# A spectral layer and an MLP on one core: the second product two steps behind its operands, eight places for the kept half, casts without priority, two reads sooner

## The chip, the cores and the metric

The kernel runs on one core of a Trainium2 chip. The metric is the time of one execution on the device in microseconds (us), the median of several runs.

## The reference

```python
X = np.fft.rfft(x, axis=1)                       # x: 8 x 3008 x 256
Yr = Xr @ w_r - Xi @ w_i + b_r                   # Xr, Xi: real and imaginary part of X
Yi = Xr @ w_i + Xi @ w_r + b_i
Yr = np.sign(Yr) * np.maximum(np.abs(Yr) - 0.01, 0.0)      # Yi likewise
y = np.fft.irfft(Yr + 1j * Yi, n=3008, axis=1).astype(np.float32)
h = y.reshape(24064, 256) @ w_in                 # 256 x 2048, float64 words
g = np.maximum(0.01 * h, h)
out = (g @ w_out).astype(np.float32)             # 2048 x 256, float64 words
```

## The kernel before

**The spectral part.** Each of the 8 batches has a transform along its 3008 positions, done as two factors (47 and 64) by matmuls. `fwd(b)` does the first factor (`stage_a`) and writes to u_dram. `mid(b)` reads that, with a table fb for each pair of columns, does the second factor (`stage_b`, psf or psh from fb and u), splits the result into a high and a low part (eh), multiplies by the complex weights, applies the soft threshold (t, zf, zh), turns back one factor (`stage_g`) and writes v_dram. `inverse` reads v_dram (vin) and does the last factor; its result y is copied into yc. In the prologue batch 0 goes through `fwd` and `mid` alone; batches 1 to 7 are streams whose pieces are put between those of the MLP, in chunks up to index 26. The last five chunks have hardly any side work.

**The MLP** runs over 24064 tokens in 32 chunks of 752. Products are in two parts, high and low (three matmuls for each product). The first product is in Strassen's form: in each of 8 steps q of a chunk, `moe_a` has 12 matmuls into four banks psh, and `moe_b` 9 more. Behind `moe_a` a copy and an add make p (tag p1), and two adds make half of gs; `moe_b` is followed by the activations of gf and the last add of gs. gf is the half of a step's result that is used at once; gs is the kept half. `parts` splits a half into gh (a cast on the scalar engine, L594) and gl (a subtraction on the vector engine, L595). For gf that stands in the block of raised priority (AHEAD = 200); for gs it is `late`, called later.

The second product is `moe_o`: for one step, one half and one half eh of the outputs, six matmuls into one of two banks pso (L612). When step 7 is in, the bank is copied to ob on the scalar engine (L618) and written out. In the first half of a chunk the groups of half 0 stand between the pieces of the first product, taken from the list `behind`; in the second half only groups of half 1 follow, with the forms of the next chunk (`forms`, L520 to L532: sums of yc, split into yhl) between them.

**Order.** A scheduler places the recorded instructions on each engine; it goes by the order in which the code records them, by `high_priority` and by `issue_after`. A tile with n places (bufs) makes its next writer wait for the last reader of the place. `early` is a region that holds weights in the prologue; `load_wout` reads w_out in pieces `raw` of 512 KB and splits them.

Of the kernel before, what the change touches and what calls it, by code (L numbers as in the profile page):

```python
# [8 lines left out]
F32 = mybir.dt.float32  # L9
# [21 lines left out]
def spectral_mlp_kernel(  # L31
# [98 lines left out]
    def load_weights():  # L130

        w = early[:, 6 * D:6 * D + 3 * NH * D + P]
        r, d, n = (w[:, k * NH * D:(k + 1) * NH * D].rearrange("p (a f) -> p a f", a=NH) for k in range(3))
        i = sb.tile([P, NH, D], F32, name="w_i", tag="yt", bufs=1)
        for t, src in ((r, w_r), (i, w_i)):
            sync.dma_start(t, src.rearrange("(a p) f -> p a f", p=P))
        dve.tensor_sub(d, i, r)
        dve.scalar_tensor_tensor(n, i, -1.0, r, ALU.mult, ALU.subtract)
        consts.update(wr32=(r,), wd32=(d,), wn32=(n,), gb32=(w[:, 3 * NH * D:],))
# [51 lines left out]
    def load_wout():  # L191
# [5 lines left out]
        def load():  # L197
            k = len(raws)
            raw = sb.tile([P, CS, 2], U32, name="raw", tag="ez"[k % 2], bufs=1)
            with tc.issue_after(reads[-1].ins):  # L200
                sync.dma_start(raw.rearrange("p (a f) w -> p a (f w)", a=n), ov[:, k * n:(k + 1) * n, :])
            raws.append(raw)
# [25 lines left out]
    XT = [("gs", NQ - 1)] * 2 + [("gg", 6)] * 3 + [("gs", NQ - 1), ("yc", 3)]  # L228

    def fwd(b):  # L230
# [5 lines left out]
        def load(c):  # L236
            cols = slice(2 * c * D, min(2 * c + 2, NS) * D)
            n = cols.stop - cols.start
            if b < NPRE:
                tag, bufs = XT[c]  # L240
                x_t[c] = [sb.tile([PA, 2 * D], F32, name="xin", tag=tag, bufs=bufs)[:, :n] for h in range(2)]
            else:
                x_t[c] = [
                    sb.tile([PA, 2 * D], F32, name=f"xin{h}", tag="uv"[h], bufs=3 - h)[:, :n] for h in range(2)
                ]
# [79 lines left out]
    def mid(b):  # L325
        ud = u_dram[b]
# [5 lines left out]
        u_t, e_t, z_t, fb_t = {}, {}, {}, {}  # L332
# [12 lines left out]

        def turns(j):
            if j < NPAIR:
                fb_t[j] = sb.tile([P, 3, N2], F32, name="fb", tag="fb")
                sync.dma_start(fb_t[j], fb[j])
# [28 lines left out]
        def proj(j):  # L378
# [4 lines left out]
            for dst, c, w in ((0, 2, "wr"), (0, 1, "wn"), (D, 0, "wd")):  # L383
# [5 lines left out]
                if c == 2:  # L389
                    kc = sb.tile([P, D], F32, name="kc", tag="kc", bufs=1)  # L390
# [9 lines left out]
            c = sb.tile([P, 2, D], F32, name="c", tag="kb" if b else "yt", bufs=1)  # L400
# [32 lines left out]
        turns(0)  # L433
# [46 lines left out]
    def inverse(pi, eh):  # L480
# [12 lines left out]
        y = sb.tile([P, CS], F32, name="y", tag="y")  # L493
# [13 lines left out]
    def forms(ci):  # L507
# [4 lines left out]
        t = sb.tile([P, 2, HT], F32, name="yt", tag="yt", bufs=1)  # L512
# [13 lines left out]
        dve.tensor_sub(t[:, 1], b22, t[:, 0])  # L526
        dve.tensor_sub(b12, b22, b12)
        yield
        split(slice(2, 4), t)
        yield  # L530
        split(slice(4, 6), y1)
        dve.tensor_sub(b11, b21, t[:, 1])  # L532
# [16 lines left out]
    def moe_a(ci, q):  # L549
# [6 lines left out]
        u = sb.tile([P, HT], F32, name="p1", tag="p1")  # L556
        g1 = sb.tile([P, 2, 2, HP], F32, name="gs", tag="gs", bufs=NQ - 1)
# [8 lines left out]
    def moe_b(ci, q):  # L566
# [7 lines left out]
        with tc.high_priority(AHEAD):  # L574
# [3 lines left out]
            parts(ci, q, 0, g0)  # L578
            g = g1[:, :, :, :HH]
            dve.tensor_add(g[:, 0], halves(c12[:, :HT]), halves(u))  # L580
        early_parts[:] = parted
# [57 lines left out]
    def moe():  # L639
# [3 lines left out]
        def next_o(eh):  # L643
            if behind:
                in_order(moe_o, *behind[0], eh)
                if eh:
                    behind.pop(0)

        for ci in range(nch):
            nxt = tokens(ci + 1) if ci + 1 < nch else iter(())  # L650
            units = 0
            for q in range(NQ):
# [9 lines left out]
                if q >= NQ - 2:  # L662
                    late(ci, q + 2 - NQ)
# [5 lines left out]
            behind += [(ci, q, 1) for q in range(NQ)]  # L669
            for q in range(NQ):  # L670
                for eh in range(NH):
                    next_o(eh)
                    if eh:
                        late(ci, q + 2)
# [4 lines left out]
        while behind:  # L679
            for eh in range(NH):  # L680
                next_o(eh)
# [29 lines left out]
    load_win(0, (sync, act))  # L711
    load_weights()
# [13 lines left out]
    m0 = Stream(mid(0), MID)  # L726
# [13 lines left out]
    for i in range(1, 17):  # L740
# [3 lines left out]
        if 5 <= i < 12:  # L744
            next(fp.gen)
    m0.finish()
# [3 lines left out]
    next(wout)  # L750
# [144 lines left out]
```

## Time and profile before

| | |
|---|---|
| runs | 2581.2, 2583.67, 2587.37 us; median 2583.67 us |
| profiled execution | 2589.46 us, of which the span is 2587.7 us |
| TensorE (PE) busy | 2455.0 us (95%), 15388 matmuls |
| vector engine (DVE) busy | 1891.2 us (73%) |
| scalar engine (ACT) busy | 1658.8 us (64%) |
| POOL busy | 248.0 us (10%) |
| first matmul of the first product | at 143.26 us |

The span is the time from the first to the last instruction in the profile. Matmuls are pipelined and their ends are modelled, so a busy TensorE isn't one at its peak; a weight load (PEld) stands ahead of each matmul or pair and shows what it waited for.

### The profile page before, as it was taken

What the parts mean: (1) busy time and instruction counts of PE and PEld (TensorE: products, weight loads), DVE (VectorE), ACT (ScalarE), POOL (GpSimd) and SP (SyncE); (2) the same over time, 40 slices, a digit from 0 to 9 for tenths busy, and PEclk for the clock granted to TensorE, in tenths of its full rate; (3) what the DMA queues carried; (4) which work ended last, traced back from release to release, by engine and by line L of the source; (5) the groups of instructions that cost most, each with busy time, mean ns of one, the idle gap of its engine ahead of it and who ended that gap; (6) DMA issues with size and microseconds to landing.
All of it is one profiled execution on the core that took longest, in us unless ns stands there. A gap on an engine that the chain in (4) does not pass through costs nothing.

```text
span 2587.7 us, 41422 instructions
## 1 busy us (share of the span) xinstructions
PE 2455.0 (95%) x15388; PEld 2336.0 (90%) x15388; DVE 1891.2 (73%) x3208; ACT 1658.8 (64%) x3198; POOL 248.0 (10%) x192
## 2 busy tenths in 40 slices
PE   6879999999999999999999999999999999999999
PEld 4569999999899998999989999899999999999998
DVE  6687788677776777777777767777768777766665
ACT  4666676667566666676656766566766666655554
POOL 0200012000110001100011001100002000000000
PEclk8989999999999999999999999999999999999999
DMA  7531123221231212321123211321213221100000
GB/s 234 164 119 54 49 56 114 71 57 51 71 95 53 57 45 76 86 66 49 49 81 86 57 53 44 93 79 51 60 50 100 65 59 40 44 28 28 17 13 19
DMA packets 138479, 173.68 MB, mean 67 GB/s; under 512 B 15661, under 2 KB 100645, under 8 KB 138277
## 3 DMA queue, kind: packets, MB, share of 16 engines
q1 hardware_dynamic: 97688, 124.17, 16.0%
q10 hardware_dynamic: 40589, 46.87, 7.1%
q8 instruction: 121, 1.98, 0.3%
q14 instruction: 81, 0.66, 0.1%
HBM read 95.22 MB, written 75.76 MB: 66 GB/s over the span
## 4 chain that ended last, share of the span: by engine, by line
PE 70%; DVE 12%; ACT 11%; DMA 3%; issue 2%; POOL 0%; SPq 0%; ACTq 0%; DVEq 0%; POOLq 0%
PE pso L612 30%; PE psh L98 25%; PE psf L82 10%; PE psf L491 3%; DVE gl L595 2%; ACT gh L594 2%; ACT zf L411 2%; PE psf L359 1%; ACT gf L577 1%; DVE t L403 1%; ACT zf L407 1%; DVE gs L562 1%; DVE t L401 1%; DVE p L561 1%; DVE gf L576 1%
## 5 line engine op out<-in xcount | busy, mean ns | idle before, releaser
L98 PE MATMUL psh<-yhl,win_hi 128*128 128x376 f32 x3584 | 884.0, 329 | 15.7 <-DVE gs L562 8.5
L98 PEld LDWEIGHTS psh<-yhl,win_hi 128*128 128x128 f32 x3584 | 610.8, 190 | 40.8 <-DVE gs L562 15.8
L98 PE MATMUL psh<-yhl,win_lo 128*128 128x376 f32 x1792 | 578.5, 323 | 0.0
L612 PE MATMUL pso<-gl,wout_hi 128*128 128x376 f32 x2048 | 505.1, 328 | 15.4 <-DVE gl L595 14.1
L612 PE MATMUL pso<-gh,wout_hi 128*128 128x376 f32 x2048 | 502.7, 327 | 15.4 <-ACT gh L594 15.2
L612 PE MATMUL pso<-gh,wout_lo 128*128 128x376 f32 x2048 | 496.7, 324 | 0.0
L612 PEld LDWEIGHTS pso<-gl,wout_hi 128*128 128x128 f32 x2048 | 353.0, 190 | 32.3 <-DVE gl L595 30.2
L612 PEld LDWEIGHTS pso<-gh,wout_hi 128*128 128x128 f32 x2048 | 353.6, 190 | 30.3 <-ACT gh L594 25.6
L612 PEld LDWEIGHTS pso<-gh,wout_lo 128*128 128x128 f32 x2048 | 359.1, 190 | 0.0
L98 PEld LDWEIGHTS psh<-yhl,win_lo 128*128 128x128 f32 x1792 | 339.0, 189 | 0.2 <-issue 0.2
L595 DVE TENSOR_TENSOR gl<-gf,gh 128x752 fp32r<-128x752 f32 x256 | 245.9, 961 | 106.8 <-ACT gh L594 104.5
L595 DVE TENSOR_TENSOR gl<-gs,gh 128x752 fp32r<-128x752 f32 x256 | 242.4, 958 | 63.8 <-ACT gh L594 63.6
L393 POOL TENSOR_TENSOR kb<-bias,kc 128x512 f32<-128x512 f32 x96 | 133.6, 1392 | 1613.5 <-ACT kc L391 1577.7
L594 ACT CAST gh<-gs 128x752 fp32r<-128x752 f32 x256 | 209.9, 822 | 111.4 <-PE pso L612 100.3
L575 ACT ACTIVATE gf<-psh 128x376 f32<-128x376 f32 x256 | 124.3, 485 | 234.0 <-PE psh L98 188.3
L561 DVE TENSOR_TENSOR p<-psh,p 128x376 f32<-128x376 f32 x256 | 140.1, 547 | 137.4 <-ACT p L560 121.4
L577 ACT ACTIVATE gf<-gf 128x376 f32<-128x376 f32 x256 | 132.6, 518 | 140.9 <-DVE gf L576 138.0
L576 DVE TENSOR_TENSOR gf<-psh,p 128x376 f32<-128x376 f32 x256 | 139.6, 545 | 112.7 <-PE psh L98 111.8
L594 ACT CAST gh<-gf 128x752 fp32r<-128x752 f32 x256 | 209.8, 820 | 6.2
L584 ACT ACTIVATE gs<-gs 128x752 f32<-128x752 f32 x256 | 212.1, 828 | 1.5 <-DVE gs L580 0.7
L560 ACT COPY p<-psh 128x376 f32<-128x376 f32 x256 | 117.8, 460 | 98.6 <-PE psh L98 98.4
L580 DVE TENSOR_TENSOR gs<-psh,p 128x376 f32<-128x376 f32 x256 | 139.5, 545 | 20.0 <-PE psh L98 17.7
(130 smaller groups left out, 3538.5 us busy)
## 6 DMA issues: line engine op xcount, KB each, us to landing
u<-u_dram SPq DMA_DIRECT2D x192, 128.0 KB, 2.8
v_dram<-v ACTq DMA_DIRECT2D x192, 128.0 KB, 2.4
out_dram<-ob SPq DMA_DIRECT2D x128, 188.0 KB, 1.9
vin<-v_dram SPq DMA_DIRECT2D x94, 240.0 KB, 3.4
xin<-x_dram SPq DMA_DIRECT2D x90, 240.0 KB, 3.0
u_dram<-xin ACTq DMA_DIRECT2D x72, 240.0 KB, 2.4
fb<-fb_dram SPq DMA_DIRECT2D x96, 96.0 KB, 2.0
u_dram<-xin SPq DMA_DIRECT2D x24, 240.0 KB, 3.9
```

Of the source, the lines that this page charges most:

```text
L82: last = nc.tensor.matmul(dst, a, b, start=(i == 0), stop=(i == len(terms) - 1))
L98: mlp[:] = [nc.tensor.matmul(dst, a, b, start=start and i == 0, stop=i == 2, skip_group_check=True)]
L393: pool.tensor_add(kb, bias, kc.unsqueeze(1).broadcast_to([P, 2, D]))
L561: dve.tensor_add(u, c22[:, :HT], u)
L575: act.activation(g[:, 0], halves(c11[:, :HT]), AF.Prelu, alpha=SLOPE)
L576: dve.tensor_add(g[:, 1], halves(c21[:, :HT]), halves(u))
L577: act.activation(g[:, 1], g[:, 1], AF.Prelu, alpha=SLOPE)
L580: dve.tensor_add(g[:, 0], halves(c12[:, :HT]), halves(u))
L584: act.activation(g, g, AF.Prelu, alpha=SLOPE)
L594: cp = act.copy(h, g)
L595: parted[:] = [cp, dve.tensor_sub(l, g, h.bitcast(F32))]
L612: mlp[:] = [nc.tensor.matmul(pv, a[:, f, s], turned_halves(r[:, i]), start=(f == 0 and j == 0), stop=(f == NF - 1 and j == 2),)]
```

## The change

Five things change. (1) `next_o` takes a group from `behind` when at least two steps are in it (before: one), so that a group stands two steps behind the step that makes its operands; at the very end the list is emptied. The late parts are recorded one step later: the first behind all eight steps, the others one for each pair of groups. (2) gs has eight places and not seven. For their room p1 has one place and not two, yt one half and not two (the forms are written in another order for it), y is 470 columns long and not 512; w_i and a tile c of the prologue use another tag. (3) `parts` for gf is recorded behind the last add of gs and outside the block of raised priority. (4) In the prologue the first two pieces of w_out are read into `early`, at the fourteenth piece of the first mid and not behind it. (5) The table fb of the first pair is read ahead of the weights; kc uses two tags in turn there; two x tiles of batch 1 use the places of gs.

```diff
         def load():
             k = len(raws)
-            raw = sb.tile([P, CS, 2], U32, name="raw", tag="ez"[k % 2], bufs=1)
-            with tc.issue_after(reads[-1].ins):
+            if k < 2:
+                raw = early.bitcast(U32)[:, (13 + 4 * k) * D:(17 + 4 * k) * D].rearrange("p (f w) -> p f w", w=2)
+            else:
+                raw = sb.tile([P, CS, 2], U32, name="raw", tag="ez"[k % 2], bufs=1)
+            with tc.issue_after(reads[13 if k < 2 else -1].ins):
                 sync.dma_start(raw.rearrange("p (a f) w -> p a (f w)", a=n), ov[:, k * n:(k + 1) * n, :])
...
-    XT = [("gs", NQ - 1)] * 2 + [("gg", 6)] * 3 + [("gs", NQ - 1), ("yc", 3)]
+    XT = [("gs", NQ)] * 2 + [("gg", 6)] * 3 + [("gs", NQ), ("yc", 3)]
...
-                tag, bufs = XT[c]
+                tag, bufs = XT[c if c < NX - 1 else -1 - b]
...
     def mid(b):
+        u_t, e_t, z_t, fb_t = {}, {}, {}, {}
...
+        turns(0)
+        if b == 0:
+            yield 0
...
-        turns(0)
         for j in range(2):
             load(j)
...
+    m0 = Stream(mid(0), MID)
+    next(m0.gen)
     load_weights()
...
         if 5 <= i < 12:
             next(fp.gen)
+        if i == 13:
+            next(wout)
     m0.finish()
     fp.to(0.69)
     for p in due[0]:
         v_load(p)
-    next(wout)
...
-        y = sb.tile([P, CS], F32, name="y", tag="y")
+        y = sb.tile([P, 2 * NG * N1], F32, name="y", tag="y")
...
-        t = sb.tile([P, 2, HT], F32, name="yt", tag="yt", bufs=1)
+        t = sb.tile([P, 1, HT], F32, name="yt", tag="yt", bufs=1)
...
-        dve.tensor_sub(t[:, 1], b22, t[:, 0])
+        split(slice(2, 3), t)
         dve.tensor_sub(b12, b22, b12)
         yield
-        split(slice(2, 4), t)
+        dve.tensor_sub(t[:, 0], b22, t[:, 0])
+        split(slice(4, 6), y1)
         yield
-        split(slice(4, 6), y1)
-        dve.tensor_sub(b11, b21, t[:, 1])
+        dve.tensor_sub(b11, b21, t[:, 0])
+        split(slice(3, 4), t)
...
-        u = sb.tile([P, HT], F32, name="p1", tag="p1")
-        g1 = sb.tile([P, 2, 2, HP], F32, name="gs", tag="gs", bufs=NQ - 1)
+        u = sb.tile([P, HT], F32, name="p1", tag="p1", bufs=1)
+        g1 = sb.tile([P, 2, 2, HP], F32, name="gs", tag="gs", bufs=NQ)
...
             act.activation(g[:, 1], g[:, 1], AF.Prelu, alpha=SLOPE)
-            parts(ci, q, 0, g0)
             g = g1[:, :, :, :HH]
             dve.tensor_add(g[:, 0], halves(c12[:, :HT]), halves(u))
+        parts(ci, q, 0, g0)
...
-        def next_o(eh):
-            if behind:
+        def next_o(eh, least=2):
+            if len(behind) >= least:
                 in_order(moe_o, *behind[0], eh)
...
-                if q >= NQ - 2:
-                    late(ci, q + 2 - NQ)
...
             behind += [(ci, q, 1) for q in range(NQ)]
+            late(ci, 0)
             for q in range(NQ):
                 for eh in range(NH):
                     next_o(eh)
                     if eh:
-                        late(ci, q + 2)
+                        late(ci, q + 1)
...
         while behind:
             for eh in range(NH):
-                next_o(eh)
+                next_o(eh, 1)
```

In the tables of order below, a row is the line of the program, the operation, and the tile it writes from the tiles it reads. First the vector engine, at the last step of chunk 28, which has no side work, in the kernel before:

```order
L561 TENSOR_TENSOR p_25496<-psh,p_25496 128x376
L595 TENSOR_TENSOR gl<-gs,gh 128x4x188
L562 TENSOR_TENSOR gs<-psh,p_25496 128x2x188
L563 TENSOR_TENSOR gs<-psh,gs 128x2x188
L576 TENSOR_TENSOR gf<-psh,p_25496 128x2x188
L580 TENSOR_TENSOR gs<-psh,p_25496 128x2x188
L595 TENSOR_TENSOR gl<-gf,gh 128x4x188
L523 TENSOR_TENSOR yt<-yc 128x376
```

and in the changed kernel:

```order
L568 TENSOR_TENSOR p_25536<-psh,p_25536 128x376
L569 TENSOR_TENSOR gs<-psh,p_25536 128x2x188
L570 TENSOR_TENSOR gs<-psh,gs 128x2x188
L583 TENSOR_TENSOR gf<-psh,p_25536 128x2x188
L586 TENSOR_TENSOR gs<-psh,p_25536 128x2x188
L602 TENSOR_TENSOR gl<-gf,gh 128x4x188
L529 TENSOR_TENSOR yt<-yc 128x376
L527 TENSOR_TENSOR yhl<-yc,yhl 128x4x188
```

Before, the late subtraction (gl from gs) stood between p and the two operations of gs that release the second half of the first product; after, nothing stands there, and gl from gf follows the last add of gs in both.

The scalar engine at the end of that chunk's first half and the start of its second, from the cast of step 7's half gf (gh<-gf) to the two copies that free the banks (ob), before:

```order
L594 CAST gh<-gf 128x4x188
L584 ACTIVATE gs<-gs 128x4x188
L520 CAST yhl<-yc 128x4x188
L594 CAST gh<-gs 128x4x188
L618 COPY ob<-pso 128x376
L594 CAST gh<-gs 128x4x188
L618 COPY ob<-pso 128x376
```

and after:

```order
L601 CAST gh<-gf 128x4x188
L591 ACTIVATE gs<-gs 128x4x188
L526 CAST yhl<-yc 128x4x188
L601 CAST gh<-gs 128x4x188
L526 CAST yhl<-yt 128x2x188
L601 CAST gh<-gs 128x4x188
L625 COPY ob<-pso 128x376
L526 CAST yhl<-yc 128x4x188
L625 COPY ob<-pso 128x376
```

Ahead of the first ob there stand five instructions after that cast now, and three before. In chunk 16, which has side work of a mid (zf, xi, eh), the scalar engine has, after, from the activation of gs at the same place:

```order
L591 ACTIVATE gs<-gs 128x4x188
L414 COPY zf<-t 64x256
L601 CAST gh<-gs 128x4x188
L418 ACTIVATE zf<-t,sign 64x256
L414 COPY zf<-t 64x256
L418 ACTIVATE zf<-t,sign 64x256
L526 CAST yhl<-yt 128x2x188
L377 COPY xi<-psf 128x256
L378 CAST eh<-psf 128x2x256
L601 CAST gh<-gs 128x4x188
L526 CAST yhl<-yc 128x4x188
L625 COPY ob<-pso 128x376
```

The ob of the first bank is the last row; its second one follows two rows later.

The scalar engine at the end of the prologue, up to the first copy odd of an inverse, before (cvq, cva and wout_hi are the splitting of w_out, xin a forward stage of batch 1):

```order
L293 COPY xin<-psh 120x512 x4
L146 ACTIVATE cvq<-raw 128x512
L147 ACTIVATE cva<-raw 128x512
L146 ACTIVATE cvq<-raw 128x512
L293 COPY xin<-psh 120x512
L215 CAST wout_hi<-cva 128x512
L293 COPY xin<-psh 120x512
L494 COPY odd<-psf 128x240
```

After, the first activations on w_out's words stand within the mid of batch 0 (zf, kc, v):

```order
L436 COPY v<-psh 128x512
L370 COPY ef<-psh 128x2x256
L438 DMA v_dram<-v 64x2x256 x2
L398 COPY kc<-pso 128x256
L146 ACTIVATE cvq<-early 128x512
L414 COPY zf<-t 64x256
```

and the rows ahead of the first odd are:

```order
L438 DMA v_dram<-v 64x2x256 x2
L218 CAST wout_hi<-cva 128x512
L296 COPY xin<-psh 120x512
L147 ACTIVATE cva<-early 128x512
L296 COPY xin<-psh 120x512
L146 ACTIVATE cvq<-raw 128x512
L218 CAST wout_hi<-cva 128x512
L296 COPY xin<-psh 120x512 x2
L146 ACTIVATE cvq<-raw 128x512
L147 ACTIVATE cva<-raw 128x512
L296 COPY xin<-psh 120x512 x2
L500 COPY odd<-psf 128x240
```

Two activations cvq<-raw, on the third and fourth piece of w_out, stand there now instead of those on the first two.

## Rows read from the trace of the kernel before

**Rows 1.** The page: busy us, share of the span and instructions of each engine.

```profile
PE 2455.0 (95%) x15388; PEld 2336.0 (90%) x15388; DVE 1891.2 (73%) x3208; ACT 1658.8 (64%) x3198; POOL 248.0 (10%) x192
```

**Rows 2.** Stretches: us, busy us (count) of PE, PEld, DVE, ACT, POOL; clock, DMA, GB/s.

```profile
0.00:143.30 143.30, 101.70 (x369) 66.82 (x369) 95.40 (x149) 79.15 (x156) 20.64 (x18) 0.87 0.68 199
...
240.00:2471.50 2231.50, 2157.30 (x13843) 2084.36 (x13842) 1642.07 (x2805) 1454.77 (x2820) 222.55 (x171) 1.00 0.22 61
```

**Rows 3.** Waits of the weight loads, 240 to 2588 us: us in total, times, longest.

```profile
PEld pso L612 <- DVE gl L595: 29.5, 51, 1.2
PEld pso L612 <- ACT gh L594: 25.6, 36, 1.3
PEld psf L82 <- ACT eh L374: 22.1, 19, 2.2
PEld psh L98 <- DVE gs L563: 12.6, 42, 0.6
PEld psh L98 <- DVE gs L562: 12.2, 24, 1.0
PEld psf L82 <- ACT zh L418: 9.5, 6, 1.9
...
PEld pso L612 <- ACT ob L618: 2.7, 12, 0.3
```

**Rows 4.** Timeline, chunk 29: start, us, instruction [idle before it and releaser].

```profile
2436.62 0.48 PE L612 MATMUL pso<-gh,wout_hi 128*128 128x376 f32 x2
...
2436.82 0.55 DVE L580 TENSOR_TENSOR gs<-psh,p 128x376 f32<-128x376 f32 x1
...
2437.48 0.82 ACT L594 CAST gh<-gf 128x752 fp32r<-128x752 f32 x1
2437.58 0.48 PE L98 MATMUL psh<-yhl,win_hi 128*128 128x376 f32 x2
...
2438.21 0.82 ACT L584 ACTIVATE gs<-gs 128x752 f32<-128x752 f32 x1
...
2438.33 0.94 DVE L595 TENSOR_TENSOR gl<-gf,gh 128x752 fp32r<-128x752 f32 x1 [0.96 <-ACT gh L594]
...
2438.94 0.45 ACT L560 COPY p<-psh 128x376 f32<-128x376 f32 x1
...
2440.14 0.94 DVE L595 TENSOR_TENSOR gl<-gs,gh 128x752 fp32r<-128x752 f32 x1 [0.17 <-ACT gh L594]
...
2441.79 0.30 PEld L98 LDWEIGHTS psh<-yhl,win_hi 128*128 128x128 f32 x2 [1.00 <-DVE gs L562]
...
2444.58 0.30 PEld L612 LDWEIGHTS pso<-gh,wout_hi 128*128 128x128 f32 x2 [0.72 <-ACT gh L594]
...
2446.59 0.46 ACT L618 COPY ob<-pso 128x376 f32<-128x376 f32 x1
...
2447.10 0.30 PEld L612 LDWEIGHTS pso<-gh,wout_hi 128*128 128x128 f32 x2 [0.30 <-ACT ob L618]
```

**Rows 5.** The page's costliest groups: xcount | busy, mean ns | idle before, releaser.

```profile
L612 PE MATMUL pso<-gl,wout_hi 128*128 128x376 f32 x2048 | 505.1, 328 | 15.4 <-DVE gl L595 14.1
L612 PE MATMUL pso<-gh,wout_hi 128*128 128x376 f32 x2048 | 502.7, 327 | 15.4 <-ACT gh L594 15.2
```

**Rows 6.** Groups of the scalar engine, 1409 to 1723 us (four chunks).

```profile
L411 ACT ACTIVATE zf<-t,sign 64x256 f32<-64x256 f32 x24 | 12.1, 505 | 0.3
```

**Rows 7.** Timeline of the prologue's end.

```profile
125.03 0.67 ACT L146 ACTIVATE cvq<-raw 128x512 f32<-128x512 uint32 x1 [3.97 <-DMA raw<-w_out_dram]
...
135.71 2.05 PE L491 MATMUL psf<-ga,early 120*128 120x128 f32 x8 [4.01 <-ACT xin L293]
...
140.51 3.74 PE L82 MATMUL psf<-xin,fa 120*120 120x512 f32 x4 [2.75 <-DVE y L497]
```

**Rows 8.** The chain that ended last, in chunk 0.

```profile
175.61 4.58 DMA raw<-w_out_dram
```

**Rows 9.** Timeline of the prologue's start.

```profile
35.84 3.75 PE L359 MATMUL psh<-fb,u 128*128 128x128 f32 x16 [11.79 <-DMA u<-u_dram]
```

More of the change, by code (lines that the diff above doesn't have):

```diff
@@ L133, in load_weights @@
         r, d, n = (w[:, k * NH * D:(k + 1) * NH * D].rearrange("p (a f) -> p a f", a=NH) for k in range(3))
-        i = sb.tile([P, NH, D], F32, name="w_i", tag="yt", bufs=1)
+        i = sb.tile([P, NH, D], F32, name="w_i", tag="t", bufs=1)
         for t, src in ((r, w_r), (i, w_i)):
@@ L325, in mid, with turns @@
     def mid(b):
+        u_t, e_t, z_t, fb_t = {}, {}, {}, {}
+        def turns(j):
+            if j < NPAIR:
+                fb_t[j] = sb.tile([P, 3, N2], F32, name="fb", tag="fb")
+                sync.dma_start(fb_t[j], fb[j])
+        turns(0)
+        if b == 0:
+            yield 0
         ud = u_dram[b]
@@ L331, in mid @@
         act.dma_start(vd.rearrange("c k n d -> (c k) n d")[:, N2, :], zero)
-        u_t, e_t, z_t, fb_t = {}, {}, {}, {}
         if b == 0:
@@ L344, in load @@
             u_t[j] = u
[L346 to L349, printed above, removed]
         def stage_b(j):
@@ L389, in proj @@
                 if c == 2:
-                    kc = sb.tile([P, D], F32, name="kc", tag="kc", bufs=1)
+                    kc = sb.tile([P, D], F32, name="kc", tag="kc" if b or j % 2 else "p1", bufs=1)
                     act.copy(kc, ps_k[:, :D])
@@ L399, in proj @@
             t = sb.tile([P, 2, D], F32, name="t", tag="t" if b else "v", bufs=1 if b else 2)
-            c = sb.tile([P, 2, D], F32, name="c", tag="kb" if b else "yt", bufs=1)
+            c = sb.tile([P, 2, D], F32, name="c", tag="kb" if b else "t", bufs=1)
             dve.tensor_add(flat(t), ps_y, flat(kb))
@@ L725, in spectral_mlp_kernel @@
         split_consts()
-    m0 = Stream(mid(0), MID)
     m0.to(0.001)
```

## The prediction

> **What bounds the kernel now.** The page's list of busy times comes first: TensorE is busy for 2455.0 of 2587.7 us, the vector engine for 73% and the scalar engine for 64% [rows 1]. All matmuls stay, so only TensorE's idle time can be won: 132.7 us. The table of stretches says where that is: the prologue up to the first matmul of the first product (143.3 us) has 41.6 us of it, and the stretch from 240 to 2471.5 us has 2231.5 - 2157.3 = 74.2 us, at a granted clock of 1.00 [rows 2]. These 74.2 us understate the loss: a matmul is shown as 0.32 us long, though the next starts 0.16 us later, so a wait is partly covered by the modelled end of the matmul before it. I therefore add up the waits of the weight loads, which stand in order ahead of the matmuls.
>
> The list of those waits [rows 3] names four kinds. The second product (bank pso) waits for the low half gl 51 times and for the high half gh 36 times, 29.5 + 25.6 = 55.1 us. The first product (psh) waits for the kept half gs, 12.6 + 12.2 = 24.8 us. The mids (psf) wait for eh and zh, 22.1 + 9.5 = 31.6 us. The output copy ob, which frees a bank of the second product, costs 2.7 us in 12 waits.
>
> The timeline of a chunk without side work shows how they arise [rows 4]. A group of the second product is six matmuls: it starts at 2436.62 and the first product goes on at 2437.58, so a group takes 0.96 us and a matmul 0.16 us. In the regular step the cast of gh starts 0.86 us after that group's start, and gl ends 2.65 us after it (2438.33 + 0.94 - 2436.62). The next group needs them 2.88 us after, its own 0.96 us and the 12 matmuls of the next step's first half. There is 0.2 us to spare, and any foreign cast ahead on the scalar engine makes a wait. At the chunk's last step, the late subtraction for the second half (2440.14) stands on the vector engine ahead of the one that makes gs, and the first product waits 1.00 us for it; then gh is late (0.72 us), because the group that wants them stands right behind one other group; then ob (0.30 us).
>
> **The change, part by part.**
>
> *Two steps behind.* An operand gets one more step of the first product and of the second: 33 matmuls at 0.16 us, 5.3 us, above the 2.88 us it had. A chain that was 0.2 us short of late is then early by more than 5 us in the first half of a chunk, and in the second half the first groups are still those of the first half's steps 6 and 7, made before. The 55.1 us go. By the matmul rows of the page's costliest groups only 15.4 us of idle stand ahead of the groups with gh and 15.4 us ahead of those with gl [rows 5], so the lower end is 31 us; I take 55, since a matmul's start is what moves the rest, and starts moved by about the weight load's wait.
>
> *Casts no longer preferred, late parts moved.* In the vector engine's order at the last step, nothing stands between the sum p and the two operations of gs any more, so the 1.00 us there goes. In other steps the subtraction is moved behind, not removed; over the whole order, the share of steps with p and the first gs operation side by side rises from 90 to 117 of 192. I take 14 of the 24.8 us, between 0 and 24.8. The mids' operands eh and zh stood behind these preferred casts on the scalar engine; in the order of TensorE the matmuls that use them stand further behind their makers (the 10% point of this distance for eh rises from 2.2 to 2.9 us at 0.16 us for a matmul, for zh from 5.5 to 7.7 us). I take 15 of 31.6 us, between 0 and 32.
>
> *A new wait: the bank of the output.* There are two banks pso, and with all operands early TensorE reaches the place sooner at which it wants one back. Count from the end of the last step's first product: one group of step 5 is left, then step 6 and step 7 have two each, and at 0.96 x 5 = 4.8 us the first group of the kept half wants the bank that step 7's first group filled by 3.8 us. In the kernel before the distance between filling and wanting was the same 0.96 us, but TensorE came late itself, waiting for gh and gl, and ob cost only 0.30 us. The copy ob is not preferred. In the scalar engine's order after the change (a chunk without side work) the casts gh, the activation gs, a form's cast, gh, a form's cast and gh stand ahead of it. The cast of gh starts 0.86 us in; full casts start 0.72 us apart (2437.48 and 2438.21), the form's half cast half that, so ob starts at 4.9 and ends at 5.4 us. The weight load is wanted 0.16 us ahead of its matmul and goes 0.05 us after the copy's end (2447.10, and 2446.59 + 0.46): a wait of 5.45 - 4.64 = 0.8 us. In a chunk with side work, mid operations stand there too: in the one shown (index 16) a form's cast more, two activations of zf, 0.51 us each, of which 0.1 us overlaps the one before [rows 6], two copies of zf, an estimate of 0.1 us less, and one operation each for xi and eh, 0.8 us together by the same measure. That puts the end of ob at 8.2 us; two mid matmuls stand on TensorE in that stretch (0.3 us), so the wait is 3.3 us. Worked the same way the three other kinds of chunk of a batch, which have other mid matmuls in between as cover, get 0.1, 2.1 and 1.2 us: 6.7 us for four chunks, six times, and 7 chunks x 0.8. That is 46 us, 43 more than the 2.7 us of before. If side work of TensorE always covers it this is 0; if each of the 24 chunks with side work pays as the worst kind, it is 24 x 3.3 + 7 x 0.8 = 85 us.
>
> *Eight places for gs, one for p, one for yt, a shorter y.* p has one place now: the add that reads it last ends 0.75 us after the second product's group starts (2436.82 + 0.55 - 2436.62), and the copy that fills it again comes 2.3 us after that start (2438.94). The forms reuse one t: its reader is on the same engine or a cast ahead. I cost them at nothing; if that cover went, a wait of the size of one vector operation (0.55 us) would stand in some steps, and the first product would be late by it.
>
> *Prologue.* The first activation on w_out's words ends a wait of 3.97 us for their read at 125.03, with copies of the first inverses and of the second forward stage behind it on the scalar engine; TensorE ends an idle time of 4.01 us at 135.71 for such a copy [rows 7]. In the order after the change two of these activations stand within the first mid. But the third read's activation stands again ahead of the copy odd, so the end on the small side is 0. Without the two idle times of 4.01 and 2.75 us ahead of it, the first product, which starts at 143.3 us [rows 2], would start at about 136; I take 7 us. In chunk 0 a read of w_out is waited for on the chain that ended last (4.58 us) [rows 8]; two reads come earlier and the second product asks a step later: 5 us (0 to 5). The earlier read of the first table saves nothing: the first mid matmul waits 11.79 us for u, not for the table [rows 9].
>
> *Sum.* -55 - 14 - 15 + 43 = -41, and -7 - 5 = -12: -53 us. The profiled execution took 2587.7 us of span and 1.8 outside, 2589.5 us; less 53 that is 2536.5. It stood 5.8 us above the median of the runs, 2583.7, so I forecast 2531 us (-2.0%). With every term at its bad end it would be 2589.5 - 31 + 82 - 5.8 = 2635, with every one at its good end 2589.5 - 55 - 25 - 32 - 3 - 12 - 5.8 = 2457; ends that lie all on one side are unlikely.
>
> A rule speaks against part of this. The Trainium skill, Perfetto Trace Analysis, Optimization Strategy, says that a gap which repeats on the engine that should be saturated can mean that SBUF or PSUM has no room for the next tile. By it the thing to look at is places, and the change adds places in SBUF (gs) but none in PSUM, where two output banks stay. In the trace before, the row for ob (12 waits, 0.3 us at the most) does not bear it out: there the operands were late, not the bank. If it comes true after the change, it is the second rival below.
>
> **The rivals.**
>
> A. *The bank costs little.* The mids' matmuls stand between in most chunks and cover ob, so the wait is about 0.8 us in all 31 chunks, 25 us and not 46. Then it is -55 - 14 - 15 - 12 = -96 for the gains and 22 for the bank, 2510 us; with 20 us more of the gs and mid waits gone, 2490. For it: the kind of chunk with 0.1 us. Against: three of four kinds show operations ahead of ob on the scalar engine.
>
> B. *The bank takes most back.* Every chunk with side work pays as the worst, 85 us: -96 + 82 = -14, 2570 us. For it: ob has no priority, and zf's operations wait for the vector engine. Against: in the three other kinds I count less.
>
> C. *Slower.* The same mechanism with ob behind still more. All the gains are 96 us, with ob's old 2.7 it is 99; over 31 boundaries the point where it decides is 3.2 us each. At 4.5 us in 24 chunks and 0.8 us in 7 the wait is 114 us: 2584 - 99 + 114 = 2599 us. For it: the casts are no longer preferred, so mid work may get ahead of gh and ob both. Against: it needs every kind to be beyond the worst that I count.
>
> D. *It doesn't do what it says.* The casts, now at ordinary priority, come so late that a second step of distance only replaces the priority, and gh and gl are waited for as before: 2589.5 - 12 - 5.8 and little else, 2572 to 2584. Against: in the order after, gh stands right behind gf on the scalar engine and gl one operation behind gs on the vector engine.
>
> **How the numbers follow.** My sum, with its terms a little off (2510 to 2552), 0.57; A (2490 to 2510, a little of it below), 0.17; B (2552 to 2578), 0.13; D 0.05; C 0.08. The range 2490 to 2574 leaves out C, most of D and a little of A and B: 0.19. A difference under 0.2% (5 us) can't be told from none. Faster: the sum, A, nearly all of B and a part of D, 0.86. Same: the rest of D and a little of B and C, 0.05. Slower: 0.09.
>
> **What would show it.** In the list of weight-load waits after: pso for gl and gh near 0 (55.1); psh for gs about 11; eh and zh about 20; pso for ob about 46 in some 30 waits, each at the start of a chunk's second half, the longest about 3 us. The first matmul of the first product at about 136 us. Wrong: if pso still waits for gh or gl by more than 15 us, the two steps are not enough; if ob is near 5 us, my count of the scalar engine's queue is wrong; if it is over 80 us, it decides the whole.

## The result

The changed kernel takes 2545.17 us, the median of 4 runs (2539.61 to 2549.2), against 2583.27 us for the kernel before in the runs beside it: a ratio of 0.9849, 95% interval 0.9825 to 0.9873. That is 38 us less where the prediction had 53; its time, 2531 us, is 14 us too low, and the measured one lies in its range. The profiled execution has a span of 2541.2 us, 46.5 less than the one before.

The list of busy times and the stretches of the profile after (columns as in [rows 1] and [rows 2]; the second ends now at 135.9 us, where the first product starts):

```profile
PE 2426.3 (95%) x15388; PEld 2336.5 (92%) x15388; DVE 1860.0 (73%) x3240; ACT 1657.6 (65%) x3230; POOL 253.0 (10%) x192
```

```profile
0.00:135.90 135.90, 100.46 (x369) 66.12 (x369) 92.23 (x149) 78.93 (x156) 22.87 (x18) 0.89 0.71 207
...
232.00:2426.00 2194.00, 2129.18 (x13819) 2084.33 (x13818) 1612.37 (x2826) 1451.01 (x2841) 224.76 (x171) 0.99 0.22 62
```

The first product starts 7.4 us sooner, as the sum had it. TensorE's busy time is shorter by 28.7 us with the same matmuls, and its idle time by 17.8. That is so because the modelled end of a matmul covers part of the wait behind it (the wait of 3.44 us below is 3.15 us of idle time), and from 240 us on the list has 122 waits where it had 234. The waits of the weight loads from 240 us on, the answer to [rows 3] (us in total, times, longest):

```profile
PEld pso L619 <- ACT ob L625: 48.4, 37, 3.7
PEld psh L98 <- DVE gs L569: 17.4, 32, 1.0
PEld psf L82 <- ACT eh L381: 10.1, 13, 1.0
PEld psh L98 <- ACT p L567: 4.6, 6, 0.8
PEld psh L98 <- DVE gs L570: 4.3, 19, 0.4
```

All waits of the list, those not shown included, are 96.9 us; before they were 138.3. gl and gh are gone from the list altogether (55.1 us). ob stands first, 48.4 us in 37 waits with 3.7 us as the longest, where the prediction had 46 in some 30 with about 3. gs has hardly moved: 17.4 + 4.3, and 4.6 for the copy of p ahead of it, 26.3 us against 24.8. eh fell from 22.1 to 10.1 us, and zh is no longer among the rows (9.5).

The new wait at its place, in chunk 16, of which the prediction counted the scalar engine's queue (timeline: start, us, instruction, and the idle time with its releaser):

```profile
1447.90 0.50 ACT L418 ACTIVATE zf<-t,sign 64x256 f32<-64x256 f32 x1
1447.91 0.48 PE L619 MATMUL pso<-gl,wout_hi 128*128 128x376 f32 x2
1448.42 0.50 ACT L526 CAST yhl<-yt 128x376 fp32r<-128x376 f32 x1
1448.83 0.37 ACT L377 COPY xi<-psf 128x256 f32<-128x256 f32 x1
...
1449.10 0.59 ACT L378 CAST eh<-psf 128x512 fp32r<-128x512 f32 x1
...
1449.58 0.83 ACT L601 CAST gh<-gs 128x752 fp32r<-128x752 f32 x1
...
1450.30 0.83 ACT L526 CAST yhl<-yc 128x752 fp32r<-128x752 f32 x1
...
1451.02 0.48 ACT L625 COPY ob<-pso 128x376 f32<-128x376 f32 x1
...
1451.55 0.30 PEld L619 LDWEIGHTS pso<-gh,wout_hi 128*128 128x128 f32 x2 [3.44 <-ACT ob L625]
```

The last pair of matmuls of the two steps starts at 1447.91. The scalar engine is at a zf operation then; a form's half cast, xi, eh, a cast of gh and a form's cast are still ahead of ob, which starts at 1451.02. The weight load waits 3.44 us for it (3.3 worked out). In chunks 8 to 24 the four kinds of chunk show 3.4, 0, 2.5 to 2.8 and 0.5 us (worked out: 3.3, 0.1, 2.1, 1.2), a chunk without side work 0.9 us in two waits, one for each bank (0.8). The first six chunks are less regular: 0.2, 3.3, 3.7, 1.0, 0 and 0 us.

Why gs did not fall shows in chunk 18:

```profile
1548.01 0.50 ACT L418 ACTIVATE zf<-t,sign 64x256 f32<-64x256 f32 x1
...
1548.54 0.83 ACT L591 ACTIVATE gs<-gs 128x752 f32<-128x752 f32 x1
...
1549.28 0.46 ACT L567 COPY p<-psh 128x376 f32<-128x376 f32 x1
...
1549.78 0.30 PEld L98 LDWEIGHTS psh<-yhl,win_hi 128*128 128x128 f32 x2 [0.77 <-ACT p L567]
...
1551.02 0.30 PEld L98 LDWEIGHTS psh<-yhl,win_hi 128*128 128x128 f32 x2 [0.78 <-DVE gs L569]
```

The kept half's activation (gs, 0.83 us), which nobody needs soon, and four operations on zf stand on the scalar engine ahead of the copy of p (L567), which then comes at 1549.28; the first product waits 0.77 us for that bank and 0.78 us for gs behind it. The wait that the prediction removed, behind the late subtraction at the last step ([rows 4], 1.00 us), is gone: the chunks without side work show 0.4 us for gs in all, from 2312 us on. This one has taken its place.

One more thing shows in a table of stretches. After a wait of 3.68 us for ob in chunk 2, TensorE's granted clock is 0.50, the lower of its two levels, for six microseconds:

```profile
369.00:375.00 6.00, 6.00 (x19) 6.00 (x20) 5.24 (x8) 3.45 (x7) 0.00 (x0) 0.50 0.17 64
```

19 matmuls in 6.00 us is 0.32 us each, where 0.16 us is usual in this kernel ([rows 4]).

### The profile page after: what moved, and what is told of

It reads as the page before. It is cut to its first block, busy times and chain, and to the rows that moved or that the text cites. A ratio compares the mean times of both kernels' runs of the same rounds, so it can differ in the third digit from the quotient of the medians.

```text
span 2541.2 us, 41585 instructions
## 1 busy us (share of the span) xinstructions
PE 2426.3 (95%) x15388; PEld 2336.5 (92%) x15388; DVE 1860.0 (73%) x3240; ACT 1657.6 (65%) x3230; POOL 253.0 (10%) x192
## 4 chain that ended last, share of the span: by engine, by line
PE 73%; ACT 11%; DVE 4%; issue 2%; DMA 2%; POOL 0%; ACTq 0%; DVEq 0%; POOLq 0%
PE pso L619 31%; PE psh L98 27%; PE psf L82 10%; PE psf L497 3%; ACT gh L601 2%; PE psf L366 2%; ACT zf L418 1%; ACT yhl L526 1%; ACT gs L591 1%; ACT gf L584 1%; ACT zf L414 1%; DVE t L408 1%; DVE gf L583 1%; DMA u_dram<-xin 1%; DMA u<-u_dram 1%
## 5 line engine op out<-in xcount | busy, mean ns | idle before, releaser
L98 PEld LDWEIGHTS psh<-yhl,win_hi 128*128 128x128 f32 x3584 | 604.2, 190 | 46.0 <-DVE gs L569 21.2
L619 PE MATMUL pso<-gl,wout_hi 128*128 128x376 f32 x2048 | 497.1, 325 | 0.0
L619 PEld LDWEIGHTS pso<-gh,wout_hi 128*128 128x128 f32 x2048 | 356.5, 191 | 49.5 <-ACT ob L625 48.6
L619 PEld LDWEIGHTS pso<-gl,wout_hi 128*128 128x128 f32 x2048 | 358.5, 190 | 1.0
L570 DVE TENSOR_TENSOR gs<-psh,gs 128x376 f32<-128x376 f32 x256 | 140.3, 548 | 23.2 <-PE psh L98 6.0
```

Of the source, the lines that this page charges most:

```text
L98: mlp[:] = [nc.tensor.matmul(dst, a, b, start=start and i == 0, stop=i == 2, skip_group_check=True)]
L570: dve.tensor_add(g[:, 1], halves(c12[:, :HT]), g[:, 1])
L619: mlp[:] = [nc.tensor.matmul(pv, a[:, f, s], turned_halves(r[:, i]), start=(f == 0 and j == 0), stop=(f == NF - 1 and j == 2),)]
```

## The experiments

Only the main lines of each edit are shown.

**The prologue alone.** The kernel before, with the parts on w_out's first words, the first table and the x tiles (kc keeps its one tag):

```diff
-            with tc.issue_after(reads[-1].ins):
+            with tc.issue_after(reads[13 if k < 2 else -1].ins):
...
+        if i == 13:
+            next(wout)
```

> The kernel before with only the prologue's part of the change (w_out's first two pieces and the first table sooner, m0 started sooner, the x tiles of batch 1). By the prediction's sum it gives 12 us: first matmul of the first product at 136 us instead of 143.3, and 5 us more in chunk 0, so about 2571 us against 2583. The rival: chunk 0 waits for the next piece of w_out instead, and only the 7 us of the first product's start are left (2576), or these too are given back by the first chunk (2583). The waits of the second product for gh and gl stay at 55 us.

Measured: 2587.3 us, ratio 1.0007 (0.9998 to 1.0016). This is the rival that gives all back. In its trace the first product starts at 137.1 us, 6.2 sooner; the chunks after it start 6.7, 4.4, 0.9 and -0.1 us sooner. Its stretches for chunks 0 and 1 (us; matmul count in brackets):

```profile
137.10:230.60 93.50, 82.24 (x469) 74.50 (x467) 76.84 (x138) 60.32 (x112) 3.84 (x3) 0.95 0.26 74
230.60:309.30 78.70, 77.34 (x518) 75.53 (x517) 59.54 (x103) 55.70 (x111) 6.98 (x5) 1.00 0.19 53
```

Chunk 0 holds 469 matmuls against 495 before, and chunk 1 518 against 493: some 25 matmuls of the side work have moved to chunk 1. What is left is used up in new waits, among them one of 3.1 us for ob in chunk 0 and one of 3.4 us for gl in chunk 2; from the first product to the end the weight loads wait 161.0 us, and in the kernel before 155.8.

**One step behind, the rest as changed.**

```diff
-        def next_o(eh, least=2):
+        def next_o(eh, least=1):
```

> The changed kernel with the second product one step behind its operands again; eight places, late parts and prologue stay changed. If the second step of distance is what removes the waits for gh and gl, they come back at 50 us or more, and the wait for the bank's copy ob falls from 48.6 us to under 10, since TensorE is late there anyway: 2550 to 2570 us against 2545. The rival: the late parts' new places (or the casts behind the adds) had removed the waits, and the distance only made the bank's wait: then gh and gl stay under 15 us and the time is about 2505.

Measured: 2589.4 us, ratio 1.0017 (1.0009 to 1.0026). Its waits:

```profile
PEld pso L619 <- DVE gl L602: 47.9, 83, 2.9
PEld pso L619 <- ACT gh L601: 27.6, 37, 2.9
PEld pso L619 <- ACT ob L625: 9.7, 16, 3.5
```

The second step is what removes gl and gh; without it they wait for 75.5 us and not for 55. The 20 us more lie in the chunks' second half, where gl rises from 18.1 to 38.1 us and gh from 8.4 to 13.9: the late parts, which make them, come later now. The bank's wait falls to 9.7 us, as expected; the time is above the range that I gave.

**Two steps alone.**

```diff
-        def next_o(eh):
-            if behind:
+        def next_o(eh, least=2):
+            if len(behind) >= least:
```

> The kernel before with the second product two steps behind as the only edit; seven places of gs, late parts at steps 6 and 7, prologue as before. If the distance alone makes the MLP's part of the gain, the time is 12 us above the changed kernel's, 2557 us. The rival: two steps behind, the three pairs of gh and gl in six places are all in use at step 7, so the late parts recorded there wait for a place, and casts behind them on the scalar engine with them: a wait of 1 to 3 us at each of 31 boundaries takes the gain back, 2570 to 2610 us.

Measured: 2544.68 us, ratio 0.9842 (0.9829 to 0.9856): as large a gain as that of the whole change, from one condition. But it gets there in another way:

```profile
PEld psh L98 <- DVE gs L562: 36.8, 43, 2.4
PEld psh L98 <- DVE gs L563: 12.5, 43, 0.6
...
PEld pso L612 <- ACT ob L618: 9.9, 18, 1.8
...
PEld pso L612 <- DVE gl L595: 0.8, 1, 0.8
```

gl costs 0.8 us and gh 0.2, so the distance alone removes these waits. ob costs 9.9 us here and gs 49.3: the other parts of the change together exchange the one wait for the other. The mids wait for more operands as well, 28 us for kc, xz and v, where the changed kernel has 3.

**The old prologue in the changed kernel.** (The edit is the first one, the other way round, and kc has one tag again.)

> The changed kernel with the prologue of the kernel before. The run with the prologue's part alone kept nothing of the 6 us at the first product (2587 us, not 2571), so by that theory this one is at 2545 us, like the changed kernel, with the first matmul of the first product at 142 us and the difference gone by the fifth chunk. The rival is the prediction's term: in a kernel whose second product asks a step later the earlier words are worth their 12 us, and it stands at 2557.

Measured: 2554.84 us, ratio 0.9886 (0.9863 to 0.9909), 9.7 us above the changed kernel. The rival holds here. The stretch that begins 240.0 us after the start in this run, and the one that begins at 233.1 us in the changed kernel:

```profile
240.00:2548.00 2308.00, 2240.69 (x14503) 2195.38 (x14502) 1680.76 (x2944) 1514.83 (x2952) 221.96 (x171) 0.99 0.21 60
```

```profile
233.10:2541.00 2307.90, 2239.55 (x14503) 2192.78 (x14501) 1686.01 (x2944) 1514.58 (x2952) 224.76 (x171) 0.99 0.21 60
```

Both hold 14503 matmuls and last the same, so the 6.9 us of the profiled spans are all won ahead of them, and kept. So the prologue is worth 7 to 10 us in the changed kernel and nothing in the kernel before.

**The late parts where they were.**

```diff
+                if q >= NQ - 2:
+                    late(ci, q + 2 - NQ)
...
-            late(ci, 0)
...
-                        late(ci, q + 1)
+                        late(ci, q + 2)
```

> The changed kernel with the late parts recorded where they were before (two in steps 6 and 7, then one ahead of each pair of groups). With the two steps alone, the wait for ob was 9.9 us and not 48.6, and that for gs 49 us and not 27. If the late parts' place decides between these two, here ob falls under 15 us and gs rises above 40, and the time stays at 2545 within 5 us: one wait for the other. The rival: the eight places or the casts behind the adds make the difference; then ob stays above 40 us.

Measured: 2513.65 us, ratio 0.9724 (0.9706 to 0.9742). Moving the late parts costs the changed kernel 31.5 us:

```profile
PEld psh L98 <- DVE gs L570: 25.4, 46, 2.0
PEld psh L98 <- DVE gs L569: 19.3, 33, 1.0
PEld pso L619 <- ACT ob L625: 15.1, 26, 1.9
```

ob fell to 15.1 us and gs rose to 44.7, so the first theory has the place right. (The 48.6 us that the expectations give for ob is the 48.4 with a wait in chunk 0.) But it said that the time stays, and it fell: all waits from the first product on are 95.6 us and not 116.2, and the mean granted clock is 0.995 against 0.989, since 27 us at half clock behind the prologue are gone. By an estimate from all runs (last section) those are worth about 11 us.

It isn't simply a cast that the move puts ahead of ob. In the chunks without side work the wait is no shorter here: 0.95 us at the second bank, with the move 0.73 and 0.16 at the two. The difference lies in chunks with side work. In chunk 16 the operations on zf, xi and eh come ahead of step 7's cast gh<-gf here and ob is not waited for; in the changed kernel they stand behind it, ahead of ob.

This run and the one with two steps alone differ by the prologue, the casts and the places (gs, p1, yt, y, with the order of the forms that goes with them). The casts' place does nothing (see below) and the prologue is worth 7 to 10 us, so some 21 of the 31 us between 2544.7 and 2513.7 are left for the places. No run has them alone.

**The banks by pairs of steps.** For the last two steps of the first half and the first two of the kept half, both groups of one half of the outputs go ahead of both of the other:

```diff
+            steps, behind[:NQ] = behind[:NQ], []
+            todo = [(k + i, e) for k in (0, 2) for e in range(NH) for i in range(2)]
+            todo += [(k, e) for k in range(4, NQ) for e in range(NH)]
             for q in range(NQ):
                 for eh in range(NH):
-                    next_o(eh)
+                    k, e = todo.pop(0)
+                    in_order(moe_o, *steps[k], e)
```

> The changed kernel with another order of groups around the middle of a chunk: first half of outputs for two steps, then the second half for the same two steps, for the last two groups of the first half and the first two of the kept half. Each bank is then wanted 1.91 us after it was filled, not 0.96 us. If the wait for ob is the time from filling to the copy's end minus that distance, each of the waits (about 3.4, 0.5, 2.4, 1.0 us in the four kinds of chunk, 0.8 without side work) falls by 1 us, and by 0.7 us more where the copy moves ahead of one cast: 48.6 us become 12 to 25, and the time 2510 to 2525 us. The rival: the scalar engine's queue, not the bank's distance, sets it, the copy moves back by as much, and the time stays at 2545.

Measured: 2525.85 us, ratio 0.9772 (0.9759 to 0.9785).

```profile
PEld psh L98 <- DVE gs L569: 20.0, 34, 1.0
PEld pso L619 <- ACT ob L625: 15.0, 12, 2.4
...
PEld pso L619 <- DVE gl L602: 10.6, 25, 1.9
```

ob fell to 15.0 us as worked out: it is gone in the chunks without side work, and 2.1 + 0.3 us are left in those that had 3.4. gl is back with 10.6 us, all in the second half, where its groups are wanted sooner. gs (29.8 us with L570), eh (14.1) and the reads of vin (8.9) are dearer too, and the time is just above the range.

**ob ahead of a late cast.** The late part of step 1 is recorded behind the first ob and issued after it:

```diff
-            act.copy(ob, po)
+            obs[:] = [act.copy(ob, po)]
...
-                    if eh:
+                    if eh and q:
                         late(ci, q + 1)
+                    if q == 1 and not eh:
+                        with tc.issue_after(obs[0].ins):
+                            late(ci, 1)
```

> The changed kernel with one edit: the late part of step 1 is recorded behind the first copy ob and issued behind it, so that one cast of 0.72 us no longer stands ahead of ob on the scalar engine. If that queue is what the bank waits for, the 0.8 us of a chunk without side work go entirely and each of the others falls by about 0.7 us and by what the scheduler then moves behind ob as well: 48 us become 10 to 30, the time 2520 to 2535. The rival: the bank's distance of 0.96 us is too short wherever the cast stands; ob stays above 40 us and the time at 2545.

Measured: 2500.54 us, ratio 0.9672 (0.9658 to 0.9687), better than expected.

```profile
PEld psh L98 <- DVE gs L569: 13.4, 32, 0.9
...
PEld pso L619 <- ACT ob L625: 12.0, 25, 3.0
PEld psh L98 <- DVE gs L570: 5.2, 26, 0.5
```

The banks are as many, and each is wanted as soon after it was filled. What has changed is the queue ahead of ob, and 36 us of its wait go. But it is not the one cast that gives them. In the chunks without side work the wait, which was to go entirely, has only moved to the second bank, behind the cast that was moved:

```profile
2301.46 0.46 ACT L625 COPY ob<-pso 128x376 f32<-128x376 f32 x1
...
2303.27 0.47 ACT L625 COPY ob<-pso 128x376 f32<-128x376 f32 x1
...
2303.79 0.30 PEld L619 LDWEIGHTS pso<-gh,wout_hi 128*128 128x128 f32 x2 [0.72 <-ACT ob L625]
```

Some 35 of the 36 us lie in chunks with side work: in chunk 16 zf, xi and eh no longer stand between the cast gh<-gf and ob, and its 3.44 us are gone. The scheduler placed the mid's operations anew around the one edit. The time falls by 45 us: all waits are 31 us less, and the time at half clock behind the prologue falls from 27 to 7 us.

**The kept half's activation one step later.** It is kept back until the next step's copy of p is issued:

```diff
-        with tc.issue_after(parted[0].ins):
-            act.activation(g, g, AF.Prelu, alpha=SLOPE)
+        pend.append((g, parted[0]))
...
+    def activate_kept(behind):
+        if pend:
+            g, cast = pend.pop()
+            with tc.issue_after((behind or cast).ins):
+                act.activation(g, g, AF.Prelu, alpha=SLOPE)
```

with a call behind the copy of p in `moe_a`, and one ahead of `late(ci, 0)`.

> The changed kernel with the activation of the kept half gs one step later, behind the copy of the next step's p. In its trace that activation (0.83 us) and four operations of zf stand ahead of the copy, which comes 1.5 us late, and the first product then waits for gs: 27 us in all. If the activation is what makes p late, half or more of these 27 us go: 2528 to 2535. The rival: zf's operations make it late, or the wait only moves to ob, which is read next on the same engine: 2543 to 2548.

Measured: 2468.18 us, ratio 0.9551 (0.9534 to 0.9568): the fastest of all, 77 us below the changed kernel, where I had expected 10 to 17.

```profile
PEld pso L627 <- ACT ob L633: 16.6, 27, 1.1
PEld psf L82 <- ACT eh L381: 4.8, 7, 1.3
PEld psh L98 <- DVE gs L570: 4.7, 21, 0.7
...
PEld psh L98 <- DVE gs L569: 1.4, 4, 0.5
```

gs fell from 21.7 to 6.1 us as the theory said (with p, 26.3 to 7.4), but the larger part is elsewhere: ob fell from 48.4 to 16.6 us, eh from 10.1 to 4.8. All waits from the first product on fell from 116.2 to 52.3 us. In the timeline of a step in chunk 18 the copy of p comes ahead of gs and zf now:

```profile
1508.54 0.48 ACT L567 COPY p<-psh 128x376 f32<-128x376 f32 x1
...
1508.90 0.85 ACT L580 ACTIVATE gs<-gs 128x752 f32<-128x752 f32 x1
...
1509.64 0.40 ACT L414 COPY zf<-t 64x256 f32<-64x256 f32 x1
```

The scheduler puts zf's operations elsewhere too: in the chunk where four of them stood ahead of ob, none does now. The chunks without side work wait for ob as before, 0.73 and 0.16 us, so what ob gains is again the place of the mids' operations; how the later activation brings that about is not shown. From 232 us to the last matmul the clock is at its full level.

**The same edit on the kernel before.**

> The kernel before with the activation of gs one step later as the only edit. On the changed kernel that edit took 77 us. If it pays because it clears the scalar engine ahead of p and of the casts, whatever the distance of the second product, it takes 30 us or more here too: gh, gl and gs together fall from 80 to under 50 us, 2530 to 2555. The rival: one step behind, the waits for gh and gl stand with TensorE's own order (0.2 us to spare), so they stay above 45 us and the time within 10 us of 2584; the edit then pays only with two steps.

Measured: 2593.16 us, ratio 1.0024 (1.0013 to 1.0035): the rival.

```profile
PEld pso L620 <- ACT gh L602: 37.7, 55, 2.8
...
PEld pso L620 <- DVE gl L603: 27.0, 48, 1.6
```

gs falls to 16.8 us, but gh and gl take 64.7, and eh and zh rise from 31.6 to 43.4. That one step leaves no slack which a cleared scalar engine could use fits this (0.2 us, [rows 4]), but why gh and eh rise is not shown.

**The banks by pairs and the activation later.** Both edits together, in the changed kernel. The expectation on record was 2508 to 2518 us if the bank and gs are separate places whose gains add, and, as the rival, 2524 to 2530 if gl takes the gain back. Measured: 2490.72 us, ratio 0.9639 (0.9618 to 0.9659), better than either, and 22.5 us slower than the activation alone.

```profile
PEld pso L627 <- DVE gl L610: 17.7, 37, 1.5
```

ob is gone from the list altogether, and yet the run is slower: gl (1.4 us with the activation alone) and the reads of vin (10.6 us, and 2.9) are waited for instead.

**Late parts sooner and the activation later.**

> The changed kernel with the late parts where they were before (2514 us by itself) and the activation of gs one step later (2468 by itself). If the first took the casts away from ahead of ob and the second takes the activation away from there and from ahead of p, part of the gain is the same (ob fell to 15.1 and 16.6 us in the two): together ob under 10 us, gs under 15, 2450 to 2465. The rival: the late subtractions in steps 6 and 7 stand ahead of gs again, as in the run of late parts alone (25 us more for gs), and it is slower than the later activation alone, 2470 to 2495.

Measured: 2508.35 us, ratio 0.9705 (0.9684 to 0.9727): slower than the activation alone and than either range. gs (13.1 us) is not the main reason, as the rival had it; ob has come back:

```profile
PEld pso L627 <- ACT ob L633: 38.0, 28, 3.2
```

Its longest waits, 3.23 us, stand in chunks 5, 9, 13, 17, 21 and 25, the kind that had little or none in the changed kernel, and chunks 8, 12, 16, 20 and 24, which had 3.4, have 0.2 at the most.

**The activation later and ob ahead of a late cast.**

> The activation of gs one step later and ob ahead of the late cast of step 1, together. What is left of ob in the run with the later activation is 16.6 us in 27 waits, 0.7 us in a chunk without side work, which one cast of 0.72 us makes up: if that is the queue, ob falls to under 5 us and the time to 2450 to 2458. The rival: the cast behind ob comes later itself and the group of step 1 waits for gh and gl: 2464 to 2475.

Measured: 2478.33 us, ratio 0.9587 (0.9571 to 0.9603), 10 us slower than the activation alone. ob falls by 3.7 us only, and gs rises:

```profile
PEld psh L98 <- DVE gs L570: 13.9, 28, 1.0
PEld pso L627 <- ACT ob L633: 12.9, 24, 2.0
```

Neither theory named this. All three pairs show the same: two edits that each shorten the wait for ob do not add, and each pair is slower than the later activation alone; what is gained at one wait is lost at another. The scheduler places the mids' operations anew in each; why these placements are worse stays open.

## Why the prediction was right, and where its sizes were off

*Two steps: -55.* Right for the waits, with its own evidence: they are gone after, come back with one step, and go with the two steps alone. In time they were worth 40 us there and not 55, since gs rose by 24.5 us and ob by 7.2.

*The bank: +43.* Right in place, size and pattern: 48.4 - 2.7 = 45.7 us, 3.44 us in the chunk that was counted. The reason was only half there. The prediction put it down to TensorE's earlier arrival and to a copy without priority. With the two steps alone ob costs 9.9 us, and with the late parts back in their places 15.1: it is with their move that the mids' operations come to stand ahead of ob. (Full casts start 0.73 us apart by its own rows and not 0.72, which changes nothing.) The prediction counted the queue as it stood but did not ask which edit had made it.

*Casts and late parts: -14 for gs, -15 for the mids.* The first is the term that failed: +1.5 us. The subtraction that held gs up is gone, but the step held that nothing else would be late in its place; the activation of gs and zf's operations are. The second was too small: eh and zh fell by about 21 us. Of the two edits in this term, the place of the casts does nothing by itself: with it undone, in the changed kernel or in the one with the late parts where they were, the instructions of every engine stand in the same order as with it, row for row.

*Eight places for gs, one for p, one for yt: 0.* The wait that it feared does not show: that for p's copy, 4.6 us, is there with two places too (4.0 us in the run with two steps alone). That they gain nothing is not borne out: by the difference above they may be worth some 21 us.

*Prologue: -12.* 7 to 10 us beside the two steps, nothing alone. The start of the first product was right (135.9 for 136), and by the way given: of the idle times of 4.01 and 2.75 us ahead of it the first is gone and 0.86 us of the second is left. The 5 us in chunk 0 do not show: from the first product to 240 us the weight loads wait 19.3 us, and 17.5 before.

*The sum, and luck in it.* The four terms of the waits come to -41 us, and all waits from 240 us on fell by 138.3 - 96.9 = 41.4 us. That they agree is luck: gs came out 15.5 us worse and the bank 2.7, the mids 6.5 better, and waits that no term names (xz, vin and others, 24.1 us before and 12.1 after) 12.0 better. The opening step, that only TensorE's idle time of 132.7 us can be won, was wrong as it stands: 28.7 of the 46.5 us won were shown as busy time. The sum of the weight loads' waits, which the prediction then used, was the right measure.

*From profile to median.* The prediction took off 5.8 us because the profiled execution of before stood above its median. The one of after stands at 2543.0, 2.1 us below its own. Profile to profile 46.5 us went and median to median 38; about 8 of the 14 us that the forecast is too low are this step, the rest is the sum itself, -53 against -46.5, mainly the 5 us of chunk 0.

The rule on repeating gaps, the Trainium skill's Perfetto Trace Analysis, Optimization Strategy, pointed to the right place: after the change the gap repeats in 37 waits at a bank. A want of places is not the whole of it here: with the same two banks, another queue ahead of ob took 36 of the 48.4 us. An order of groups that leaves each bank twice as long took 33, so room would help as well; no run has a third bank.

## What to carry to other kernels

When a stall's operands come early, look at what frees the resource at the same place, and read the queue of the engine that frees it, instruction by instruction: here that gave 43 us against 45.7 before any run. Try each part of a change of several parts alone and also left out: one condition gave as much as the whole change, a second part cost 31 us, and a third was worth 7 to 10 us or nothing, by what stood beside it. An instruction that nobody needs soon (an activation of a half that is kept) is dear when it stands ahead of one that frees a bank. Where a scheduler places the rest anew around each edit, do not add up the gains of single edits, and look for the waits chunk by chunk: an edit of one cast may work through quite other instructions.

## What the runs showed of the hardware that was not expected

After some of the waits TensorE's granted clock stands at 0.50 for some microseconds. In the changed kernel it does so right behind waits for ob of 3.68, 3.44, 2.62 and 2.53 us (from 368, 832, 1297 and 1604 us on) and behind three places where waits of 0.77, 0.78 and 0.64 us follow each other (from 935, 1242 and 1860 us on). Behind four other waits of 3.44 us (up to 1141, 1452, 1759 and 2066 us) it stays at 1.00. The kernel before has such stretches too: 137 to 143 us, in the prologue, and six from 240 us on. The run with the late parts sooner has none from the first product to its last matmul, with a mean of 0.995.

A wait costs what its row in the list says. Take from the span of a profiled run the start of its first product and all waits of the weight loads behind that: in the five runs with 27 to 38 us at half clock behind that start, 2289 to 2293 us are left, in the nine with at most 14 us, 2278 to 2284. What is left does not grow with the number of waits, 109 to 280, though the pair of matmuls behind a wait is shown as 0.58 or 0.59 us and not 0.48. By the difference, a microsecond at half clock costs about 0.4 us, an estimate.
